# A planned attention and feed-forward kernel: the softmax of its first two tiles in two parts by heads

## Chip, cores and metric

The kernel runs on one core of a Trainium2 chip. The metric is the device time of one execution in microseconds, lower is better. All times below are microseconds unless a unit is given.

## What is computed

```python
# q, k, v: (8 batches, 8 heads, 576 tokens, 64); w_in (512, 2048), w_out (2048, 512), all float32
k_p = k.reshape(B, H, 72, 8, D).mean(axis=3)           # keys and values pooled by 8: 72 of each
v_p = v.reshape(B, H, 72, 8, D).mean(axis=3)
scores = scale * np.matmul(q, k_p.transpose(0, 1, 3, 2))
scores = scores - np.max(scores, axis=-1, keepdims=True)
attn = np.exp(scores)
attn = attn / (np.sum(attn, axis=-1, keepdims=True) + 1e-09)
attn_out = np.matmul(attn, v_p)                        # -> x: (4608 tokens, 512)
h = x @ w_in
sp = np.maximum(h, 0.0) + np.log1p(np.exp(-np.abs(h)))
out = (h * erf(sp)) @ w_out
```

## The kernel before

The 4608 tokens are nine chunks of 512. Attention goes by units of 256 tokens, two tiles of 128 each (`unit`, with `softmax_tile` for the tiles and `part` for the products with the values). Eight heads are held as four pairs (`NP` = 4), two heads of a pair in the two halves of the 128 partitions.

For a batch, `keys` loads five transfers and sums each over the 8 tokens of a pool on VectorE (L594): one of 256 KB for each of the four pairs, with that pair's first 64 pooled keys, and a last one of 128 KB with the remaining 8 pooled keys of all pairs (L605). The tile `ks` keeps them under five keys of dependence, 0 to 3 for the pairs and 4 (`NP`) for the last 8. `values` does the same for the values, on VectorE or GpSimd (L590, L592), and makes the rounded values `vb` with their remainders (L618, L622).

`softmax_tile` loads a query tile (L644, 256 KB), multiplies it with the pooled keys (`scores`, 32 small matmuls, L653) into two PSUM banks, one for each half of the heads, takes from each bank the maximum over 72 keys (L661) and subtracts it (L677) on VectorE, runs one sigmoid over all 576 columns on ScalarE (L681; with a bias of -20 it is an exponential), sums over the keys (L683), inverts (L688) and multiplies (L691, on VectorE or GpSimd). Two copies (`bb`, through L450 or L451) gather the columns left over, then the tile is transposed on TensorE (L698 for the four pairs, L699 for bb) and copied back as `et` (L708, L710) and `etb` (L715, L716). `part` multiplies them with the values (L746 with et, L752 with etb and vb), and for chunk 0 the results are split into a rounded part on ScalarE (L766) and a remainder on VectorE (L767), the tiles x.

For the feed-forward part each weight tile of 128x512 comes as 64-bit floats (L501, 512 KB), is converted by ScalarE (`cv`, L504), ScalarE or GpSimd (`low`, L508, L510) and VectorE (L512), and split into a rounded part and a remainder (`halves`, L450, L451, L462). Matmuls of weights run three products for each pair of operands (`three`, `pairs`, L819). Chunk 0 goes through w_in directly (`plain_in`): the first four weight tiles have their matmuls in two halves of 256 tokens, so that the first unit's x suffices to begin. The other chunks go through a product scheme with fewer multiplications, two chunks at a time, with sums of weights and activations that the vector engines make.

The order of all this is not that of the code. `op` notes each operation with its engine, an estimated cost, a priority (its due time) and what it reads, writes and holds; a dependence can be on a whole buffer or on one key of it. `Program.order` places the operations eight times, each time with priorities from the last placing's latest times, keeps the shortest, then moves priorities around at places that the numbers in `MOVES` draw (each is a seed of a local random shift), and emits the result. Every engine's queue, SyncE's with all transfers included, gets its order from there, and runs it in order. Where the plan leaves TensorE idle in the first 57 us, small matmuls on the constants fill in (`filler`, L1129). A changed operation, due time or list of seeds therefore changes the order in the whole kernel.

Of the kernel before, what the change touches and what calls it, by code (L numbers as in the profile page):

```python
# [402 lines left out]
def moe_attention(ctx: ExitStack, tc: tile.TileContext, cst, qa, kl, vl, wi, wo, out):  # L403
# [30 lines left out]
    def dve(n):  # L434
        return 1.15 * (n + 66) / 0.96
# [162 lines left out]
    def keys(b, base):  # L598

        ks = keys_of[b] = buf("ks", [NP, SP])  # L600
        n = P * D * POOL
        for p in range(NP):
            load_pool(kl[b, n * p:n * p + n], lambda p=p: ks.ap[:, p, :D], (ks, p),
                      base + KEYS + KEYS_R * p, "k", (D,))
        load_pool(kl[b, n * NP:], lambda: ks.ap[:, :, D:], (ks, NP), base + KEYS + KEYS_R * NP, "k", (NP, SP - D))  # L605
# [19 lines left out]
    def unit(ck, u0, tiles, parts, moment):  # L625
# [9 lines left out]
        def softmax_tile(at, r):  # L635
# [13 lines left out]
            def scores():  # L649
                for p in range(NP):  # L650
# [518 lines left out]
```

## Time and profile before

| | |
|---|---|
| time, median of 3 runs | 783.02 (782.98 to 784.59) |
| profiled execution | 783.03, its span 781.3 |
| TensorE (PE) busy | 774.1, 99% |
| VectorE (DVE) busy | 640.1, 82% |
| ScalarE (ACT) busy | 544.8, 70% |
| GpSimd (POOL) busy | 438.9, 56% |
| bytes moved by DMA | 207.66 MB, mean 266 GB/s |
| granted TensorE clock | 1.0 of full speed in all slices |

The span is the time from the first to the last instruction of the profiled execution; about 1.7 us lie around it. A busy time is the union of an engine's instructions, and for TensorE it holds the fillers as well as the work. Shares over the whole span hide that the start is another stage than the rest: up to some 26 us the first two tiles of attention and the first weights are made ready, and from there matmuls of weights follow each other. The rows further down are therefore mostly of the first 26 us.

### The profile page before, as it was taken

Reading aid. Unit: us, or ns where it says so; the run is one execution under the profiler, and the core shown is the slowest. Engines: PE = TensorE matmul, PEld = TensorE weight load, DVE = VectorE, ACT = ScalarE, POOL = GpSimd, SP = SyncE. Lnnn points to the kernel's source line nnn. Section 1 sums busy time; section 2 is a strip of 40 time slices with the busy share of each in tenths; the row PEclk is TensorE's granted clock in tenths of the full one; section 3 lists DMA queues with packets and bytes.
Section 4 is the critical chain, followed back from the end, with each engine's and each line's share of the span. In section 5 each row is a group of like instructions: output and inputs, shape, how many; then the busy total and the mean of one; then the engine's idle time right before and its main releaser. Section 6 shows DMA issues by size and latency. Waiting matters only on the chain.

```text
span 781.3 us, 15278 instructions
## 1 busy us (share of the span) xinstructions
PE 774.1 (99%) x5206; PEld 665.1 (85%) x5206; DVE 640.1 (82%) x1101; ACT 544.8 (70%) x843; POOL 438.9 (56%) x413
## 2 busy tenths in 40 slices
PE   8999999999999999999999999999999999999998
PEld 6888887888888888888888888888888888888887
DVE  6999998778888896798888898877899876667982
ACT  3999986798865752899766436879855447988730
POOL 4989892578586800476653733757916404561710
PEclk9999999999999999999999999999999999999999
DMA  9989999999999899983384889644546797447551
GB/s 332 377 279 317 347 328 359 363 346 349 353 332 385 284 374 328 386 278 135 117 320 142 258 269 361 240 162 162 190 162 197 247 296 269 137 166 264 177 188 55
DMA packets 125293, 207.66 MB, mean 266 GB/s; under 512 B 12320, under 2 KB 44448, under 8 KB 125216
## 3 DMA queue, kind: packets, MB, share of 16 engines
q1 hardware_dynamic: 125216, 206.69, 76.5%
q8 instruction: 42, 0.69, 0.4%
q14 instruction: 35, 0.29, 0.1%
HBM read 160.50 MB, written 46.14 MB: 264 GB/s over the span
## 4 chain that ended last, share of the span: by engine, by line
PE 95%; DMA 2%; ACT 1%; SPq 0%; DVE 0%; POOL 0%; issue 0%; DVEq 0%; ACTq 0%
PE o L819 43%; PE h L819 42%; PE att L746 2%; PE att L653 2%; PE att L752 2%; PE att L698 2%; DMA d<-wi 1%; DMA d<-wo 1%; DMA v<-vl 1%; PE att L1129 1%; PE att L699 1%; SPq L582 0%; POOL bb L451 0%; ACT cv L504 0%; DVE m L661 0%
## 5 line engine op out<-in xcount | busy, mean ns | idle before, releaser
L819 PE MATMUL o<-gl,w 128*128 128x512 f32 x1536 | 341.6, 381 | 0.0
L819 PEld LDWEIGHTS o<-gl,w 128*128 128x128 f32 x1536 | 287.5, 189 | 41.6 <-POOL w L462 0.4
L819 PE MATMUL h<-x,w 128*128 128x512 f32 (+1 forms) x1392 | 298.1, 373 | 0.0
L819 PEld LDWEIGHTS h<-x,w 128*128 128x128 f32 x1392 | 254.1, 189 | 34.7
L846 POOL TENSOR_TENSOR g<-d,g 128x512 f32<-128x512 f32 x73 | 93.5, 1299 | 103.5 <-ACT d L842 54.2
L450 ACT ACTIVATE gl<-g 128x512 fp32r<-128x512 f32 x183 | 108.5, 624 | 51.1 <-DVE g L989 22.1
L462 DVE TENSOR_TENSOR gl<-g,gl 128x512 fp32r<-128x512 f32 x149 | 114.9, 799 | 4.2 <-ACT gl L450 3.0
L462 POOL TENSOR_TENSOR gl<-g,gl 128x512 fp32r<-128x512 f32 x59 | 85.0, 1445 | 53.6 <-ACT gl L450 53.2
L926 DVE TENSOR_TENSOR g<-t,h 128x512 f32<-128x512 f32 x96 | 65.4, 684 | 29.1 <-PE h L819 28.5
L989 POOL TENSOR_TENSOR g<-g 128x512 f32<-128x512 f32 x37 | 65.2, 1762 | 25.3 <-ACT gl L450 11.5
L842 ACT ACTIVATE d<-d 128x1024 f32<-128x1024 f32 x72 | 73.5, 1052 | 0.5
L838 ACT ACT_TABLE_LOAD x46 | 59.0, 1283 | 17.8 <-PE h L819 13.6
L838 ACT ACTIVATE d<-g 128x512 f32<-128x512 f32 x103 | 59.1, 622 | 3.8 <-DVE g L926 3.5
L926 DVE TENSOR_TENSOR t<-t,h 128x512 f32<-128x512 f32 x57 | 39.1, 686 | 27.6 <-PE h L819 25.3
L450 ACT ACTIVATE x<-xr 128x512 fp32r<-128x512 f32 (+2 forms) x51 | 27.9, 565 | 36.9 <-DVE xr L793 33.4
L842 ACT ACT_TABLE_LOAD x41 | 52.6, 1283 | 0.7
L819 PE MATMUL h<-x,ws 128*128 128x512 f32 x192 | 43.2, 379 | 0.0
L681 ACT ACTIVATE s<-s,cst 128x576 f32<-128x576 f32 x36 | 27.5, 772 | 22.2 <-DVE s L677 22.2
L989 DVE TENSOR_TENSOR g<-g 128x512 f32<-128x512 f32 x59 | 41.7, 715 | 0.6
L819 PEld LDWEIGHTS h<-x,ws 128*128 128x128 f32 x192 | 36.3, 189 | 5.2
L462 POOL TENSOR_TENSOR x<-xr,x 128x512 fp32r<-128x512 f32 (+2 forms) x16 | 22.0, 1392 | 25.7 <-ACT x L450 25.7
L451 POOL TENSOR_SCALAR bb<-s 128x64 f32<-128x64 f32 x33 | 11.8, 365 | 42.1 <-DVE s L691 28.8
(107 smaller groups left out, 973.2 us busy)
## 6 DMA issues: line engine op xcount, KB each, us to landing
w<-ws SPq DMA_DIRECT2D x192, 256.0 KB, 4.9
w<-wo SPq DMA_DIRECT2D x128, 256.0 KB, 3.7
w<-wi SPq DMA_DIRECT2D x96, 256.0 KB, 5.3
ws<-ws SPq DMA_DIRECT2D x64, 256.0 KB, 5.0
v<-vl SPq DMA_DIRECT2D x40, 256.0 KB, 5.3
q<-qa SPq DMA_DIRECT2D x36, 256.0 KB, 5.2
out<-f SPq DMA_DIRECT2D x35, 256.0 KB, 2.6
k<-kl SPq DMA_DIRECT2D x32, 256.0 KB, 5.4
```

What stands on the lines that cost most here:

```text
L450: op("ACT", act(n), prio, lambda: nc.scalar.activation(dst(), src(), AF.Copy, scale=scale), *access, turn=turn, alt=("POOL", 0.833 * n + 1 ...
L462: both(True, dve(n), gps(n), prio + 0.1, lambda e: e.tensor_sub(lo(), src(), f32(hi())), reads + [hikey], [lokey])
L653: nc.tensor.matmul(pss[x].ap[r0:r0 + 64, SP * p:SP * p + SP], raw.ap[h:h + 64, p, r0:r0 + 64], ks.ap[h:h + 64, p], start=p == 0, stop=True ...
L681: op("ACT", act(H * SP) + 93, r + 0.8, lambda: nc.scalar.activation(s.keys[:T], s.keys[:T], AF.Sigmoid, bias=bias[0][:T], scale=1.0 / 64.0 ...
L698: nc.tensor.transpose(pa.ap[:, P * p:P * p + T], s.keys[:T, p, SP - 64:SP + 64], ident[:T, :T])
L746: nc.tensor.matmul(pd.ap[64 * y:64 * y + 64, 256 * i:256 * i + n], vs.ap[h, p], et.ap[h, p, es], start=i == 0, stop=False, skip_group_chec ...
L819: nc.tensor.matmul(o, u, v, start=first and q == 0, stop=last and q == 2, skip_group_check=True)
L838: nc.scalar.activation(y(k), hs[k][0].ap, AF.Softplus)
L842: op("ACT", act(1024), prio + 0.2, lambda k=k: nc.scalar.activation(ys[k].ap, ys[k].ap, AF.Erf), own[2 * k:2 * k + 2], own[2 * k:2 * k + 2 ...
L846: both(True, dve(512), gps(512), prio + 0.3, lambda e, k=k, h=h: e.tensor_mul(h.ap, y(k), h.ap), [own[k], h], [h])
L926: op("DVE", dve(512), prio, lambda: nc.vector.tensor_add(dst.ap, u.ap, o.ap), [u, o], [dst])
L989: both(True, dve(512), gps(512), prio, lambda e: e.tensor_sub(out.ap, u.ap, v.ap), [u, v], [out])
```

## The change

For the first unit of chunk 0 alone (tiles 0 and 1), the softmax is done in two parts of two head pairs each. The score matmuls become two operations of 16, the first of which depends on the keys 0, 1 and 4 of `ks` and the second on 2, 3 and 4; maxima and subtractions become eight passes of 144 columns in place of four of 288 (two maxima and two subtractions in each part); the sigmoid becomes two of 288 columns, and the sum over keys two. The inversion and all behind it stay whole. Banks, maxima, probabilities and sums get keys of dependence by part, so that a part's operations need not wait for the other's.

For batch 0 the due time of the last 8 keys' transfer is half a step earlier: 3.5 steps in place of 4, where the pairs have 0 to 3. And `MOVES` has a new list of seeds, longer than the old, so that the order of all engines is another one in the whole kernel.

```diff
-    43000190, 43000454, 43000917, 43001956, ...
+    41000008, 41000438, 41001345, 41006004, ...
...
-        load_pool(kl[b, n * NP:], lambda: ks.ap[:, :, D:], (ks, NP), base + KEYS + KEYS_R * NP, "k", (NP, SP - D))
+        load_pool(kl[b, n * NP:], lambda: ks.ap[:, :, D:], (ks, NP), base + KEYS + KEYS_R * (NP if b else 3.5), "k", (NP, SP - D))
...
+            split = 2 if first and u0 == 0 and not on_act else 1
+            w = NP // split
+
+            def scores(p0=0, p1=NP):
+                for p in range(p0, p1):
...
+            if split == 1:
+                op("PE", 550, r, scores, [raw, *(ks for ks, _ in rows)], pss, [s, m, z],
+                   turn="q", step=True)
+            else:
+                for p0 in range(0, NP, w):
+                    op("PE", 550 / split, r + 0.1 * p0, lambda p0=p0: scores(p0, p0 + w),
+                       [raw, *((ks, e) for ks, _ in rows for e in (*range(p0, p0 + w), NP))],
+                       [(ps, p0) for ps in pss], [s, m, z], turn="q", step=True)
+            for g, p0 in [(g, p0) for p0 in range(0, NP, w) for g in range(2)]:
+                ps, q = pss[g], r + 0.1 * p0
+                pv = lambda ps=ps, p0=p0: ps.ap[:T, SP * p0:SP * (p0 + w)].rearrange("p (h k) -> p h k", k=SP)
+                gs = slice(4 * g + p0, 4 * g + p0 + w)
+                bk, mk, sk = (ps, (m, g), (s, g)) if split == 1 else ((ps, p0), (m, (g, p0)), (s, (g, p0)))
+                op("DVE", dve(w * SP), q + 0.4, lambda pv=pv, gs=gs: nc.vector.tensor_reduce(
+                    m.ap[:T, gs], pv(), AX.X, ALU.max), [bk], [mk])
...
+                    op("DVE", dve(w * SP), q + 0.5, lambda pv=pv, gs=gs, g=g, p0=p0: nc.vector.tensor_sub(
+                        s.keys[:T, p0:p0 + w, SP * g:SP * g + SP], pv(), m.ap[:T, gs].unsqueeze(2).broadcast_to([T, w, SP])),
+                       [bk, mk], [sk])
+            if split > 1:
+                for p0 in range(0, NP, w):
+                    ps_, q = slice(p0, p0 + w), r + 0.1 * p0
+                    both_ = [(s, (g, p0)) for g in range(2)]
+                    op("ACT", act(2 * w * SP) + 93, q + 0.8, lambda ps_=ps_: nc.scalar.activation(
+                        s.keys[:T, ps_], s.keys[:T, ps_], AF.Sigmoid, bias=bias[0][:T], scale=1.0 / 64.0), both_, both_, funcs="sigmoid")
+                    op("DVE", dve(2 * w * SP + 8), q + 1.0, lambda ps_=ps_: nc.vector.tensor_reduce(
+                        z.ap[:T].rearrange("t (x p) -> t p x", x=2)[:, ps_], s.heads[:T, ps_], AX.X, ALU.add), both_, [(z, p0)])
+            elif not on_act:
```

## Rows read from the trace of the kernel before

**Rows 1.** The page, busy time, share of the span and instructions of each engine.
```profile
PE 774.1 (99%) x5206; PEld 665.1 (85%) x5206; DVE 640.1 (82%) x1101; ACT 544.8 (70%) x843; POOL 438.9 (56%) x413
```

**Rows 2.** Busy us (count) by stretch: PE, PEld, DVE, ACT, POOL; clock; DMA share; GB/s.
```profile
25.79:777.50 751.71, 750.95 (x4910) 646.35 (x4907) 619.98 (x1057) 531.23 (x814) 423.97 (x384) 1.00 0.77 264
...
8.00:17.00 9.00, 9.00 (x187) 7.73 (x186) 7.88 (x20) 3.82 (x7) 6.56 (x12) 1.00 1.03 397
17.00:26.00 9.00, 8.94 (x90) 7.34 (x89) 8.67 (x20) 8.49 (x22) 8.08 (x10) 1.00 1.04 398
```

**Rows 3.** The fillers' line: durations in ns, first and last start.
```profile
L1129 PE MATMUL att<-cst x127: 272/273/421, 2.6 to 25.2; 128*128 128x256 bf16 x127
```

**Rows 4.** Timeline of TensorE: start, length, line, tiles, count.
```profile
8.09 0.73 PE L653 MATMUL att<-ks,q 64*64 64x72 f32 x32
...
18.55 0.33 PE L699 MATMUL att<-cst,bb 128*128 128x128 f32 x1
18.72 2.02 PE L1129 MATMUL att<-cst 128*128 128x256 bf16 x17
20.67 1.09 PE L746 MATMUL att<-et,vs 64*64 64x256 f32 x16
21.70 0.73 PE L752 MATMUL att<-etb,vb 64*128 64x256 f32 x8
...
25.79 2.92 PE L819 MATMUL h<-x,w 128*128 128x256 f32 x24
```

**Rows 5.** Three of SyncE's issues, and KB and us to landing of the same three.
```profile
3.54 0.43 SPq L644 DMA_DIRECT2D q<-qa  x1
...
9.26 0.33 SPq L501 DMA_DIRECT2D d<-wi  x1
...
10.09 0.33 SPq L501 DMA_DIRECT2D d<-wi  x1
...
q<-qa SPq DMA_DIRECT2D x1, 256.0 KB, 4.2
...
d<-wi SPq DMA_DIRECT2D x1, 512.0 KB, 8.2
...
d<-wi SPq DMA_DIRECT2D x1, 512.0 KB, 8.6
```

**Rows 6.** VectorE: timeline, then groups by shape from 5 to 26 us.
```profile
6.11 1.65 DVE L594 TENSOR_REDUCE ks<-k 128x64 f32<-128x512 f32 x3 [0.73 <-DMA k<-kl]
...
11.21 0.82 DVE L661 TENSOR_REDUCE m<-att 128x4 f32<-128x288 f32 x2 [0.65 <-PE att L653]
...
13.81 0.71 DVE L683 TENSOR_REDUCE z<-s 128x8 f32<-128x584 f32 x1
...
24.70 1.09 DVE L767 TENSOR_TENSOR x<-att,x 128x256 fp32r<-128x256 f32 x3
...
L594 DVE TENSOR_REDUCE ks<-k 128x64 f32<-128x512 f32 x6 | 4.0, 681 | 0.7 <-DMA k<-kl 0.7
...
L594 DVE TENSOR_REDUCE ks<-k 128x32 f32<-128x256 f32 x1 | 0.4, 408 | 0.0
```

**Rows 7.** Timeline of ScalarE.
```profile
16.09 0.76 ACT L681 ACTIVATE s<-s,cst 128x576 f32<-128x576 f32 x1
17.51 0.66 ACT L504 ACTIVATE cv<-d 128x512 f32<-128x512 f32 x1 [0.66 <-DMA d<-wi]
18.09 0.41 ACT L450 ACTIVATE bb<-s 128x64 f32<-128x64 f32 x2
...
19.85 0.36 ACT L715 CAST etb<-att 128x256 fp32r<-128x256 f32 x1
```

**Rows 8.** Timeline of GpSimd.
```profile
14.56 2.29 POOL L691 TENSOR_TENSOR s<-s,z 128x576 f32<-128x576 f32 x2
...
18.89 0.73 POOL L622 TENSOR_TENSOR vb<-vm,vb 128x256 fp32r<-128x256 f32 x1 [0.59 <-ACT vb L450]
...
24.84 2.53 POOL L462 TENSOR_TENSOR w<-f,w 128x512 fp32r<-128x512 f32 x2
```

More of the change, by code (lines that the diff above doesn't have):

```diff
@@ L647, in softmax_tile @@
             pss = [bank("att") for _ in range(2)]
-            def scores():
-                for p in range(NP):
+            split = 2 if first and u0 == 0 and not on_act else 1
+            w = NP // split
+            def scores(p0=0, p1=NP):
+                for p in range(p0, p1):
                     for ks, r0 in rows:
@@ L654, in scores @@
                                              ks.ap[h:h + 64, p], start=p == 0, stop=True, skip_group_check=True)
-            op("PE", 550, r, scores, [raw, *(ks for ks, _ in rows)], pss, [s, m, z],
-               turn="q", step=True)
-            for g, ps in enumerate(pss):
-                pv = lambda ps=ps: ps.ap[:T, :4 * SP].rearrange("p (h k) -> p h k", k=SP)
-                gs = slice(4 * g, 4 * g + 4)
-                op("DVE", dve(4 * SP), r + 0.4, lambda pv=pv, gs=gs: nc.vector.tensor_reduce(
-                    m.ap[:T, gs], pv(), AX.X, ALU.max), [ps], [(m, g)])
+            if split == 1:
[13 more added lines that the diff above has]
+                    m.ap[:T, gs], pv(), AX.X, ALU.max), [bk], [mk])
                 if on_act:
@@ L676, in softmax_tile @@
                 else:
-                    op("DVE", dve(4 * SP), r + 0.5, lambda pv=pv, gs=gs, g=g: nc.vector.tensor_sub(
-                        s.keys[:T, :, SP * g:SP * g + SP], pv(), m.ap[:T, gs].unsqueeze(2).broadcast_to([T, NP, SP])),
-                       [ps, (m, g)], [(s, g)])
-            if not on_act:
+                    op("DVE", dve(w * SP), q + 0.5, lambda pv=pv, gs=gs, g=g, p0=p0: nc.vector.tensor_sub(
[10 more added lines that the diff above has]
+            elif not on_act:
                 op("ACT", act(H * SP) + 93, r + 0.8, lambda: nc.scalar.activation(
```

44 rows, old and new, of the table MOVES are left out of this document.

## Prediction

> **What bounds the kernel now.** The reader should look at the page's first part, then at TensorE's busy time by stretch, then at the engines' timelines ahead of the first weight matmul. The page has TensorE busy for 99% of the span [rows 1], which by itself would leave nothing to win. But 127 of its matmuls are fillers, small products on the constants that the planner puts into gaps, and they all lie before 25.5 us [rows 3]. By stretch: from 25.79 us, where the first matmul of the weights starts, to 777.5 us TensorE is busy 750.95 of 751.71 us [rows 2], and from there to the end of the span of 781.3 us lie 3.8 us for the last sums and their store. So the span is three pieces: 25.79 us of start, 751.7 us of full TensorE, 3.8 us of tail. The change removes no product of the second piece and touches nothing of the third. What it can win is in the first, and there the question is what the matmul at 25.79 us waits for.
>
> Followed back: that matmul starts as VectorE's last x remainder ends (24.70 + 1.09 = 25.79 us) [rows 4, 6]. The x tiles come from products at 20.67 and 21.70 us, which need the transposed probabilities of both tiles of the first unit; the later of the two transposes is at 18.55 us, and between it and 20.67 us stand 17 fillers [rows 4]. It was held by the small copies bb on ScalarE at 18.09 us, and those stood in the queue behind a weight conversion (cv) that sat idle 0.66 us for its transfer: issued at 9.26 us, 8.2 us to landing, so 17.4 us [rows 5, 7]. The copies' own input, tile 1's scaled probabilities, was done about a microsecond earlier: GpSimd's two multiplications run 14.56 to 16.85 us, tile 0's and then tile 1's [rows 8]. Those follow the two softmaxes, which is what the change splits.
>
> **The change, part by part.** *Tile 1, where the split alone decides.* Now its maxima start at 11.21 us and its sums end at 13.81 + 0.71 = 14.52 us [rows 6]; between lie four passes of 288 columns on VectorE, one sigmoid of 0.76 us on ScalarE [rows 7], and the sums. The trace has no pass of 144 columns. Its bounds: half of the 0.41 us that a pass of 288 takes (two maxima take 0.82 us), so 0.20 us; and that with the fixed part on top, which two sizes of one reduction give: 681 ns for 512 columns, 408 for 256, so 135 ns for none [rows 6], 0.34 us in all. I take 0.22, near the lower end, because passes back to back overlap in the trace: three key sums of 681, 681 and 408 ns are done in 1.65 us. The sigmoid's half is taken as 0.43 us (an operation of 256 columns on that engine takes 0.36 us) [rows 7] and the half sums as 0.41 (the 256-column reduction). Then: scores of the first half end 0.33 us earlier (somewhat less than half of the 0.73 us of 32 matmuls [rows 4], as the last one's way through is not halved), so VectorE starts at 10.88 and ends its four passes at 11.76; the second half's passes end at 12.64 while ScalarE does the first half; second sigmoid 12.73 to 13.16; second sums 13.25 to 13.66. Against 14.52 that is 0.85 us earlier; with 0.34 us a pass it is no gain, with 0.20 it is 1.0.
>
> *Tile 0 and the keys.* Its scores start at 8.09 us. The five key sums end at 6.11 + 1.65 = 7.76 us and the query tile lands at 3.54 + 4.2 = 7.7 us: both gate [rows 4, 5, 6]. Loading the last 8 keys ahead of the fourth pair moves 128 KB forward, and with the query tile ahead of the fourth pair too the first half need not wait for that pair's transfer and its sum (0.68 us); but the same six transfers still end at 7.7 us, and if a key transfer is the last of them its sum comes behind it, so the second half starts at about 8.6 us. By the chain above tile 0 then has its sums at 11.5 to 11.7 us. GpSimd, busy 6.56 of 9 us in this stretch with the sums of values [rows 2], could then multiply at some 13 us between two of them, or where it does so now, at 14.56; tile 1's follows 1.15 us later (2.29 for two), at 14.2 us, or at 15.7 as now. So tile 1's multiplication ends at 15.4 us at best and 16.85 at worst.
>
> *What follows.* ScalarE does tile 2's sigmoid at 16.09 to 16.85 us [rows 7]. If bb comes right behind it, it is done at 17.3 us in place of 18.5, and the transposes, their copies, the products at 20.67 and 21.70 and the x tiles move by 1.2 us to 24.6 us. The low values' other input, vb, is there at 18.89 + 0.73 = 19.62 us [rows 8], which is early enough. What is late next is the second weight: its remainder is the first of GpSimd's two from 24.84 us, done near 26.1 us [rows 8], and the second group of twelve 256-column matmuls would want it 1.3 us after 24.6, at 25.9. That takes 0.2 us. **Gain at the start: 1.0 us.**
>
> *What it adds.* Per split tile two more maxima, two more subtractions, one more sigmoid and one more sum, and two score groups of 16 matmuls for one of 32: 12 instructions on VectorE and ScalarE more for both tiles, no byte and no column more. VectorE's four extra passes and the extra sum cost between 5 x 0 and 5 x 0.135 us = 0.7 us a tile; by the prices taken above it is 0.23 (8 x 0.22 - 4 x 0.41 for the passes, 2 x 0.41 - 0.71 for the sums). They lie in the stretch from 8 to 17 us, where VectorE is busy 7.88 of 9 us, so its 1.1 us of idle time cover two tiles at 0.23 but not at 0.7 [rows 2]. Without that cover up to 0.3 us fall on what VectorE does next, tiles 2 and 3, whose products come only behind the first weight matmuls. I cost it at nothing.
>
> The nearest row gives at most 135 ns for one more instruction [rows 6]. The Trainium skill (Perfetto Trace Analysis, section Optimizing Scalar/DVE Operations) gives about 125 ns of overhead to a VectorE instruction on PSUM and 60 ns to one on SBUF, and advises grouping where the engine is saturated and breaking up where it is not but keeps others waiting. From its figures the two tiles would add, as an estimate, 2 x (4 x 0.125 + 0.06) = 1.1 us, all the idle time of that stretch, and a pass would take 0.27 us; tile 1's sums would then come 0.45 us earlier in place of 0.85, which still lets bb in behind tile 2's sigmoid, if that one is not late itself: 782.0 to 782.4 us. No operation of 144 columns in this trace decides it.
>
> *The order.* All operations of all engines are placed by the planner from the new list of seeds, so every queue (SyncE's transfers included) is in another order for the whole kernel. In the second piece only 0.76 us of idle TensorE is left to win [rows 2], so there a new order can hardly win and may lose some tenths; between a gain of 0.5 us (fewer changes between attention and weight products) and a loss of 2 us I take zero, because the present order shows how little a plan need lose.
>
> **Sum.** Profiled execution 783.03 us = span 781.3 us + 1.7 us around it; the median of the three runs, 783.02, is the same. 783.03 - 1.0 = **782.0 us**. With tile 1 at its bounds and the second weight where it is: 781.2 to 782.8.
>
> **Rivals.** *More comes.* If GpSimd multiplies tile 0 at 13 us and bb is placed ahead of tile 2's sigmoid, only vb at 19.62 us holds the second product, which is now at 21.70: 2.05 us earlier. For it: the second weight waits mostly in queues, its transfer is there at 17.4 us. Against it: from 17 to 26 us VectorE is busy 8.67 of 9 us and TensorE's start needs that work done [rows 2], so it must all be moved into the idle time before. 781.0 us, and 780.4 with a little from the order.
>
> *Nothing comes.* The weights, not x, set the start: the copies stay behind the conversion that waits for 17.4 us, or fillers stand ahead of the products as they do now, or the second remainder stays at 26.1 us and the first gap is just moved behind twelve matmuls. 783.0 us, within 0.4.
>
> *Slower.* ScalarE takes its queue in order, and the trace shows its place: at 17.51 us a conversion held the bb copies for a transfer that came later than planned [rows 7]. The next weight lands 8.6 us behind its issue at 10.09, so at 18.7 us [rows 5]. If the new order puts its conversion and its byte copy (an operation of the same 512 columns, 0.66 us as well) ahead of bb too, bb goes from 18.09 to 19.4 or 20.0 us, and the start of TensorE is lost with it: 1.3 to 1.9 us. It decides once the copies stand behind a second weight; the split then wins nothing. 784.9 us.
>
> *The change does not do what it says*, that is, the first tile's halves start together since the order puts the query tile last: then tile 0 gains nothing and tile 1 still has its 0.85 us; this lies within the forecast.
>
> **How the numbers follow.** Forecast 0.38, more 0.30, nothing 0.17, slower 0.15. 0.2% (1.57 us), about what a measurement of this kernel tells from no change, lies at 781.45 and 784.6. Faster: nearly all of "more" (0.28) and the forecast's lower edge (0.08), 0.36. Slower: most of its rival, 0.13. Within: 0.51. The range leaves out the deepest gains (0.08) and the dearest waits (0.12): 780.4 to 784.6 us.
>
> **What would show it.** Right: the first weight matmul between 24.4 and 25.2 us, tile 1's sums done before 14 us, bb ahead of the conversion that waits, fewer fillers than 127, and from there to the last matmul 751 to 752 us. More: that matmul below 24 us. Nothing: it stays near 25.8, or starts earlier while the stretch behind it grows by as much. Wrong altogether: an idle time of ScalarE or TensorE of over 1 us with a weight's transfer as its end, or a second piece above 753 us.

## The result, and the profile after

| | before | after |
|---|---|---|
| time, median | 783.81 (782.98 to 786.64, 4 runs) | 794.91 (791.94 to 799.49, 4 runs) |
| profiled execution, its span | 783.03, 781.3 | 791.94, 790.2 |
| first weight matmul | 25.79 | 26.41 |
| from there to the last matmul | 751.7 | 760.0 |

The ratio is 1.0134 [1.0109, 1.0159]: slower by some 10 us, far outside the range. The traced execution of after is its shortest: ten executions of it, six of them from a later run, have a middle of 793.0. The page of after, then its busy time from the first weight matmul to the last (columns as in [rows 2]):

```profile
PE 777.8 (98%) x5222; PEld 665.8 (84%) x5222; DVE 653.5 (83%) x1118; ACT 535.3 (68%) x854; POOL 398.5 (50%) x389
```

```profile
26.41:786.40 759.99, 755.09 (x4929) 647.35 (x4927) 632.79 (x1064) 523.98 (x828) 382.38 (x355) 1.00 0.76 261
```

TensorE is still busy 98% of the time. The 8.9 us between the two spans are: 0.6 of later start; 4.1 of idle time in the second piece (759.99 - 755.09 = 4.90, against 0.76 in [rows 2]); 1.9 of fillers there, 19 of them (4929 matmuls against 4910) where before had none [rows 3]; and 2.2 by which the same 4910 matmuls are busy longer, which the profile doesn't split. The tail is 3.8 us in both.

*Where along the span.* A table worked out from the starts in the traces: each matmul that isn't a filler counts with its length at full clock, and what a kernel has done by a time is taken from what before has done by then. So it is how many us of work TensorE lags behind before. It is good to some tenths, as small matmuls run side by side and their length is an estimate. (new_ kernels are the changed kernel with an edit, old_ kernels the kernel before; they come below.)

```
at (us)            26   45   60   80  160  200  300  770
after             0.7  0.9  1.9  3.8  7.8  8.6  9.3  9.1
old_split_keys    0.3  0.4  0.2  0.6  1.7  2.6  2.8  2.8
old_stores_late  -0.1  0.0 -0.2  2.8  7.1  7.1  7.6  7.3
new_stores_fill   0.8  0.9  2.2  3.8  6.7  6.5  7.1  6.7
new_fill_no_raw   0.4  0.9  1.7  3.8  6.0  5.8  6.7  6.0
new_six           0.8  0.9  2.4  2.6  6.5  7.6  8.2  8.0
new_fill_six      0.7  0.9  1.9  2.4  4.3  4.3  5.0  4.5
new_three_cures   0.8  1.1  1.1  2.6  4.5  4.3 10.2  9.7
```

Nearly all of the loss (8.6 of 9.1 us) lies ahead of 200 us, while weights are read, converted and stored; from there after keeps pace. A second traced execution of after (after_again) has 9.7 us at 200 and 10.2 at 770. The places can be read as TensorE's idle times (timeline: start, us, line, operation, tiles, shape, count, [idle before <- what ended it]):

```profile
44.94 1.38 PE L1155 MATMUL h<-cst 128*128 128x256 bf16 x11
...
69.01 0.72 PE L663 MATMUL att<-ks,q 64*64 64x72 f32 x30 [0.33 <-DVE g L875]
70.20 5.42 PE L845 MATMUL h<-x,w 128*128 128x512 f32 x24 [0.46 <-POOL w L457]
...
76.73 0.89 PE L845 MATMUL o<-gl,w 128*128 128x512 f32 x3 [0.56 <-DVE f L518]
78.16 0.70 PE L845 MATMUL o<-gl,w 128*128 128x512 f32 x2 [0.55 <-DVE et L736]
```

At 44.94 us stand 11 fillers, 1.13 us, in a gap that the plan has there; eight more stand at 151 us (the planner fills gaps of over 1.2 us behind its first 57 us too). The four waits that follow cost 2.7 us by the gaps between starts, and all end with a piece that VectorE or GpSimd makes: of a weight, an activation or a transposed tile.

*SyncE's queue.* What its issues waited for from 20 to 62 us in after (engine, line <- releaser: us in all, times, longest), then a part of its timeline, then before's load that answers to the one at 57.02 us:

```profile
SPq L507 <- ACT cv L510: 11.4, 6, 3.3
SPq L507 <- POOL low L516: 7.4, 4, 3.5
SPq L507 <- DVE g L875: 5.7, 2, 5.4
```

```profile
49.20 0.83 SPq L588 DMA_DIRECT2D v<-vl  x1
57.02 0.33 SPq L507 DMA_DIRECT2D d<-wi  x1
...
57.87 0.43 SPq L537 DMA_DIRECT2D wi<-w  x1
```

```profile
43.12 0.84 SPq L501 DMA_DIRECT2D d<-wi  x2
```

A weight as loaded (d) needs one of five places, which it shares with the activations' values. In after the 16th load of w_in stands at the head of the queue until 57.02 us, and the stores of converted weights (wi<-w, L537) wait behind it. Before issues the same load as the second of the two from 43.12 us, at 43.6 us (it lands at 48.4, in after at 61.1), and puts six stores between 44.95 and 49.7 us. By 60 us the DMA engines have moved 17.9 MB in after, 19.6 in before; from 60 to 115 us they are 0.95 to 0.99 busy in both, so what is late by then finds little idle time to catch up in (before, then after; columns as in [rows 2], the DMA share is the last but one):

```profile
40.00:60.00 20.00, 20.00 (x94) 17.53 (x93) 19.11 (x29) 19.77 (x25) 17.31 (x19) 1.00 0.79 268
60.00:80.00 20.00, 19.98 (x211) 16.18 (x210) 18.21 (x35) 19.26 (x25) 18.96 (x24) 1.00 0.98 331
```

```profile
40.00:60.00 20.00, 20.00 (x128) 17.12 (x127) 16.12 (x29) 19.47 (x26) 17.38 (x19) 1.00 0.65 231
60.00:80.00 20.00, 18.09 (x142) 15.04 (x141) 15.12 (x29) 17.86 (x25) 17.16 (x20) 1.00 0.97 328
```

Late stores hold places, and engines wait for them: from 60 to 200 us some 31 us in after, all such waits added up (the two largest), and 0.5 us in before (the last line):

```profile
POOL sw L562 <- DMA wf<-f: 12.3, 2, 6.2
POOL xr L819 <- DMA wo<-w: 9.6, 1, 9.6
```

```profile
ACT x L450 <- DMA wo<-w: 0.5, 1, 0.5
```

### The profile page after: what moved, and what is told of

Same layout as the page of the kernel before. It is cut to its first block, busy times and chain, and to the rows that moved or that the text cites. A ratio compares the mean times of both kernels' runs of the same rounds, so it can differ in the third digit from the quotient of the medians.

```text
span 790.2 us, 15324 instructions
## 1 busy us (share of the span) xinstructions
PE 777.8 (98%) x5222; PEld 665.8 (84%) x5222; DVE 653.5 (83%) x1118; ACT 535.3 (68%) x854; POOL 398.5 (50%) x389
## 3 DMA queue, kind: packets, MB, share of 16 engines
q1 hardware_dynamic: 125216, 206.69, 75.8%
## 4 chain that ended last, share of the span: by engine, by line
PE 80%; DMA 10%; ACT 3%; SPq 3%; POOL 2%; DVE 2%; issue 1%; DVEq 0%; ACTq 0%; POOLq 0%
PE o L845 38%; PE h L845 34%; DMA wo<-w 2%; PE att L663 2%; DMA d<-wo 2%; PE att L772 2%; PE att L724 2%; DMA v<-vl 1%; DMA wi<-w 1%; PE att L1155 1%; PE att L778 1%; DMA k<-kl 1%; DMA w<-wo 1%; SPq L537 1%; DMA sw<-wf 1%
## 5 line engine op out<-in xcount | busy, mean ns | idle before, releaser
L468 DVE TENSOR_TENSOR gl<-g,gl 128x512 fp32r<-128x512 f32 x153 | 123.8, 837 | 2.6 <-ACT gl L456 2.3
L468 POOL TENSOR_TENSOR gl<-g,gl 128x512 fp32r<-128x512 f32 x55 | 76.6, 1400 | 65.9 <-ACT gl L456 65.5
L1015 POOL TENSOR_TENSOR g<-g 128x512 f32<-128x512 f32 x44 | 62.3, 1419 | 22.3 <-DVE gl L468 13.6
L456 ACT ACTIVATE x<-xr 128x512 fp32r<-128x512 f32 (+2 forms) x58 | 30.7, 556 | 30.8 <-DVE xr L819 19.2
L1015 DVE TENSOR_TENSOR g<-g 128x512 f32<-128x512 f32 x52 | 38.7, 750 | 2.4 <-POOL g L1015 2.2
L600 DVE TENSOR_REDUCE ks<-k 128x64 f32<-128x512 f32 (+1 forms) x40 | 24.3, 625 | 13.5 <-DMA k<-kl 13.3
L468 DVE TENSOR_TENSOR x<-xr,x 128x512 fp32r<-128x512 f32 (+2 forms) x53 | 33.3, 661 | 0.7 <-ACT x L456 0.6
```

Source lines behind the costliest of these rows:

```text
L456: op("ACT", act(n), prio, lambda: nc.scalar.activation(dst(), src(), AF.Copy, scale=scale), *access, turn=turn, alt=("POOL", 0.833 * n + 1 ...
L468: both(True, dve(n), gps(n), prio + 0.1, lambda e: e.tensor_sub(lo(), src(), f32(hi())), reads + [hikey], [lokey])
L600: op("DVE", dve(8 * n), prio, lambda: nc.vector.tensor_reduce(to(), t.ap, AX.X, ALU.add), [t], [t, key], alt=("POOL", gps(4 * n) + gps(2 * ...
L1015: both(True, dve(512), gps(512), prio, lambda e: e.tensor_sub(out.ap, u.ap, v.ap), [u, v], [out])
```

## Experiments: the split or the order

**old_split_keys.** The order of before on all queues, with the split put into it. The 32 score matmuls of a tile stay one operation, so the first half doesn't start ahead of the fourth pair's keys as it may in after; what is split is VectorE's and ScalarE's part:

```diff
+            def step():                     # in place of the four maxima and subtractions
+                k = len(done); done.append(k)
+                if k == 0: maxima(0)
+                elif k == 1: less_max(0); expo(0)
+                elif k == 2: maxima(2)
+                else: less_max(2)
...
+    for e in ("SP", "DVE"):                 # last 8 keys ahead of the fourth pair
+        at = [i for i, o in enumerate(ops) if not isinstance(o, tuple) and o.eng == e][3:5]
+        ops[at[0]], ops[at[1]] = ops[at[1]], ops[at[0]]
```

> The order of the kernel before on every queue, with the softmax of the first two tiles in two parts by heads in the places of the whole one, and the transfer and the sum of the last 8 keys ahead of the fourth pair's. So the change without its new order. If the order made the loss (theory 1), this stays within 1 us of the kernel before, 782.0 to 783.5 us, with the first weight matmul at 24.8 to 25.8 us. If the split itself makes it (theory 2: more instructions on VectorE, which is busy to nine tenths in the start), it is 787 us or more.

**new_whole.** The order of after, each operation whole in the place of its second part:

```diff
-                    op("PE", 550 / split, r + 0.1 * p0, lambda p0=p0: scores(p0, p0 + w),
+                    op("PE", 550 / split, r + 0.1 * p0, lambda: second_of('q', scores),
```

> The changed kernel's order on every queue, with the softmax of the first two tiles whole again: each whole operation stands where the second of its two parts stood, and the keys are in the new order. So the new order without the split. Theory 1 (the order makes the loss): 791 to 798 us as the changed kernel. Theory 2 (the split makes it): 783 to 785 us.

**old_split_bb.** old_split_keys with tile 1's copies bb moved ahead of the conversion that waits:

```diff
+    act = [i for i, o in enumerate(ops) if not isinstance(o, tuple) and o.eng == "ACT"]
+    cv, bb = act[7], act[8:10]
+    o = ops.pop(cv)
+    ops.insert(bb[1], o)
```

> The kernel before with the split softmax in its places (as in the run on the split alone) and one more thing: tile 1's two copies bb stand ahead of the weight conversion that waits for its transfer at 17.4 us on ScalarE. The prediction's step had the first weight matmul come 1.0 us earlier then, with the second weight's remainder late next. If that holds: 24.8 to 25.2 us for that matmul, 782.5 to 784 us where the kernel before has some 784. If the fillers or the weights hold it all the same: 25.6 to 26.2 us.

| | this | before beside it | ratio |
|---|---|---|---|
| old_split_keys | 784.59 (10 runs) | 784.91 | 1.0000 [0.9985, 1.0016] |
| new_whole | 796.72 (4) | 784.91 | 1.0163 [1.0130, 1.0196] |
| old_split_bb | 783.95 (10) | 783.91 | 0.9997 [0.9983, 1.0011] |

The split costs nothing that the runs tell and brings nothing in before's order; the order makes the loss, with or without the split. (The profiled execution of old_split_keys, 2.6 us above that of before, is not its usual one: its ten runs and before's have the same middle.) Why the start gains nothing is in ScalarE's timelines, old_split_keys first, then old_split_bb, and in TensorE's of old_split_bb:

```profile
17.86 0.65 ACT L504 ACTIVATE cv<-d 128x512 f32<-128x512 f32 x1 [0.56 <-DMA d<-wi]
18.44 0.41 ACT L450 ACTIVATE bb<-s 128x64 f32<-128x64 f32 x2
```

```profile
17.33 0.42 ACT L450 ACTIVATE bb<-s 128x64 f32<-128x64 f32 x2
...
19.25 0.65 ACT L504 ACTIVATE cv<-d 128x512 f32<-128x512 f32 x1 [0.30 <-DMA d<-wi]
19.84 0.58 ACT L739 ACTIVATE et<-att 128x512 f32<-128x512 f32 x1
```

```profile
18.71 2.02 PE L1160 MATMUL att<-cst 128*128 128x256 bf16 x17
20.66 1.09 PE L777 MATMUL att<-et,vs 64*64 64x256 f32 x16
```

With bb 1.1 us earlier, the next conversion waits for its transfer and the copy et behind it ends at 20.42 us; the products start at 20.66 us (20.67 in [rows 4]), right behind 17 fillers, the first weight matmul at 25.90. So TensorE's own queue holds the start: between its first scores and its first weight matmul stand 99 of before's 127 fillers, the profile lists no wait of TensorE there, and it takes 17.70 us in before, 17.65 in old_split_keys and 17.54 in old_split_bb. These two runs show what the split costs. What it would win with fewer fillers no run here shows; with ScalarE's order of old_split_bb it would be some 0.2 us at the products (20.66 - 20.42, an estimate), as et isn't there earlier.

## Experiments: stores and bytes

**new_stores_early** moves ten stores of after (2.1 MB), which stand 9 to 22 places behind a load that waits, ahead of that load in SyncE's queue; **new_stores_fill** moves 74 of those between 45 and 145 us to places ahead of loads that wait for a buffer (both in the changed kernel, each store behind the operation that makes its data; the edit of the first):

```diff
+    for ahead, moved in ((44, (53, 54)), (46, (55, 57)), (51, (60, 62, 64, 66, 71, 73))):
+        for n in moved:
+            ops.remove(sp[n])
+            ops.insert(ops.index(sp[ahead]), sp[n])
```

> The changed kernel with nothing but ten stores of converted weights (2.1 MB, data ready since 18 to 36 us) moved forward in SyncE's queue: two ahead of the weight load at 45.5 us, two ahead of the one at 46.7, six ahead of the one at 57.0, which each stand in the queue waiting for a buffer while the DMA engines run empty. Theory 1 in its form that the DMA engines are the second bound from 60 to 300 us and that the new order lets them idle ahead of it: the idle time is used, so 2.1 MB at some 340 GB/s, up to 6 us, come back: 786 to 790 us against 792 to 799, with more bytes moved by 60 us. Theory 3 (VectorE's, ScalarE's and GpSimd's queues are late by their own order, transfers only follow): no change, 791 to 798.

> The changed kernel with 74 stores of weights (ready for 10 to 50 us) moved forward in SyncE's queue, from 45 to 145 us, each into a place where the next load stands waiting for a buffer; loads keep their order among themselves, stores too. The ten stores moved alone filled the gaps up to 60 us and left those behind. Theory 1: most of the loss comes back, 785 to 789 us, and 46 to 47 MB are moved by 140 us in place of 43.5. Theory 3: 791 us or more.

**old_more_dma** puts ten copies of 256 KB within the chip's memory into before, ahead of SyncE's 61st transfer:

```diff
+    for i in range(10):
+        o = Op("SP", 0, 0, lambda i=i: nc.sync.dma_start(hbm.tile([P, 512], F32, ...), qa[...]))
+        ops.insert(ops.index(sp[60]), o)
```

> The kernel before with ten transfers more of 256 KB each, from HBM to a spare place in HBM that nobody reads, in SyncE's queue ahead of its 61st transfer (58 us). They change no other queue. If the DMA engines have no slack behind 60 us (theory 1), the time grows by what the ten take, 4 to 7 us, to 787 to 790, as idle TensorE between 60 and 200 us. If they have slack there (theory 3), within 1 us of the kernel before.

**new_no_raw, old_no_raw, new_fill_no_raw** leave out the 20 stores of raw weights (wf<-f), in after, in before, and in new_stores_fill. The sums of weights made of them later read parts of the input in their place, so these kernels do less work and give another result:

```diff
-    ... lambda: nc.sync.dma_start(raw_hbm[0][ft], f.ap), [f], [RAW[0][ft]])
+    ... lambda: None, [f], [RAW[0][ft]])
```

> The changed kernel with its order, less work: the 20 stores of the weights' raw values (256 KB each, 5.2 MB, most of them between 47 and 175 us) are left out, and the sums of weights that are made of them later read 20 other tiles of the input in their place. Nothing else moves. Theory 1 (the stores that the new order lets pile up hold SyncE's queue and the SBUF places that the engines wait for): the waits for stores between 60 and 200 us go, 784 to 788 us. Theory 3 (the engines' own queues are late): 790 us or more.

> The same 20 stores left out of the kernel before, with the same other loads. A control: that kernel's TensorE is busy throughout behind 25.8 us, so theory 1 and theory 3 both say within 1 us of it; a gain of more than 2 us would say that the stores are a bound there too.

> The changed kernel with both cures for the stores at once: those of the first 145 us moved forward into the places where SyncE's queue waits for a buffer, and the 20 stores of raw weights (5.2 MB) left out, so that the sums of weights read input tiles in their place (this part of the computation is not what the reference does). If stores and the bytes behind them make most of the loss, what is left is the later start (0.7), the gap with 11 fillers (1.1) and about 1 us of stalls: 786 to 787. If the engines' own order makes the larger part, the two cures overlap and the time is no better than with the raw stores left out alone: 788.5 to 789.5.

**old_stores_late** is the other way round, before with 42 of its stores moved back:

```diff
+    behind = {57: (49, 50, 51), 59: (52,), 64: (58,), 68: (60,), 69: (62,), 72: (63, 65, 66, 67), ...}
+    for load, stores in behind.items():
+        for n in stores:
+            ops.remove(sp[n])
+            ops.insert(ops.index(sp[load]), sp[n])
```

> The kernel before, with only SyncE's queue changed: 42 stores of converted weights and of sums (256 KB each) that start between 45 and 157 us there are moved behind as many loads as they stand behind in the changed kernel, or as far as their readers allow; no engine's own order changes and no byte is added. If the place of the stores in SyncE's queue is a cause by itself, the kernel before gets slower by 2 to 5 us (786 to 789), with idle time of ScalarE, GpSimd or VectorE between 60 and 160 us that stores end, and TensorE behind by that much at 160 us. If the engines' own order is the cause and late stores only go along with it, it stays within 0.5 us of 783.9.

| | this | before beside it | ratio |
|---|---|---|---|
| new_stores_early | 794.35 (4 runs) | 784.91 | 1.0141 [1.0124, 1.0158] |
| old_more_dma | 789.48 (4) | 784.91 | 1.0066 [1.0051, 1.0081] |
| new_stores_fill | 791.09 (5) | 783.91 | 1.0095 [1.0064, 1.0127] |
| new_no_raw | 788.92 (6) | 783.91 | 1.0061 [1.0037, 1.0086] |
| old_no_raw | 782.14 (10) | 783.91 | 0.9984 [0.9968, 1.0001] |
| new_fill_no_raw | 789.29 (4) | 784.28 | 1.0065 [1.0050, 1.0080] |
| old_stores_late | 791.55 (4) | 784.28 | 1.0096 [1.0079, 1.0113] |

*Sufficient.* In before, moving stores back and nothing else costs 7 us (2 to 5 were expected), where the whole change costs 9 to 11, and it brings the engines' waits for stores with it. In its traced execution some 1.8 us of that are matmuls at a lower clock, by the gaps between starts: behind a wait of TensorE that ends at 150.67 us its granted clock was 0.58 from 152 to 154 us and 0.57 to 156, where it stayed at 1.00 in after. Its chain of waits (start, us, what) from 62.5 us, and what TensorE waits for:

```profile
62.58 5.12 DMA wi<-w
...
71.14 5.34 DMA wi<-w
...
77.23 1.27 POOL w L462
```

```profile
78.54 1.13 PE L819 MATMUL o<-gl,w 128*128 128x512 f32 x4 [2.84 <-POOL w L462]
```

A store that starts at 71.14 us ends at 76.48; only then has GpSimd a place for the rounded weight and its remainder, and TensorE, which wanted them at 75.7, stands still for 2.84 us. old_more_dma shows that bytes alone can do the like (5 us): a query tile lands late and holds TensorE for 3.85 us at 72.88.

*Not the whole.* Moved forward in after, the stores give back about 2 to 4 us (ten of them nothing: new_stores_early), left out they give back 4 to 6, and both together no more than the one: 789.3, where its rival theory (the engines' own order) stood at 788.5 to 789.5. new_stores_fill too came out at its rival's mark (791 or more), and new_no_raw between the two. In before leaving them out brings 1.3 us by the ratio, and its interval reaches to nothing. In new_stores_fill only 4.0 us of waits for stores are left, yet it is 3.8 us behind at 80 us, like after. So some 5 us (789.29 against 784.28) have another cause.

## Experiments: places of the loads, and the gap

In new_fill_no_raw the chain from 44 us on is one of loads: DVE g frees a place at 45.1, d<-wi lands 52.9, GpSimd's low frees it at 57.2, d<-wo lands 66.5, ScalarE's conversion follows, and TensorE waits at 75.8 us. **new_six** gives loads and activations a sixth place up to 80 us (place 7 of the others, whose three buffers go elsewhere), **new_fill_six** does it in new_stores_fill:

```diff
+            if first >= 377:
+                ok = [p for p in range(6) if ends.get(p, (0, 0))[0] < first and (p < 5 or (last < 545 and end < 84000))]
+                b.place = min(ok, key=lambda p: ends.get(p, (0, 0))[1])
...
+            if b.place == 5:
+                b.home, b.place = "u", 7
```

> The changed kernel with a sixth place for weights as loaded and for the activations' values (they share five of 4 KB a partition), from the 14th weight load on and up to about 80 us; three other buffers move to make room, no operation changes its place in a queue. If loads that wait for one of the five places are what makes TensorE stall at 68 to 78 us (2.7 us in four stalls), the 14th load is issued near 41 us in place of 45.5, the 16th and the second of w_out 2 to 4 us earlier than 57.0 and 60.5, the four stalls lose at least 1.5 us, and the stores queued behind these loads come earlier as well: 791 to 793.5. If the conversions' own place in the engines' order decides, the loads come earlier, the stalls stay and so does the time: 794 to 795.

> The same sixth place in the kernel whose stores of the first 145 us are moved forward (791.1 without the sixth place). If the loads' places are the second cause beside the stores, the stalls at 68 to 78 us shrink here too and the two cures add: 788.5 to 790. If stores in front of the loads take the time that the place gives, or the engines' own order decides, it stays within 0.7 us of 791.1.

**new_no_late_fillers** leaves out all 19 fillers behind 26 us (its edit is below), **new_three_cures** does it in new_fill_six. **new_no_gap** and **new_all_cures** take out the eight fillers at 151 us but only three of the 11 at 44.94, so they don't test what their expectations say:

```diff
+    for i in [i for i, o in enumerate(ops) if isinstance(o, tuple)][:123:-1]:
+        del ops[i]
```

> The changed kernel without the 11 fillers at 44.94 us (1.13 us from the first of them to the next weight matmul, whose operands were done at 42.4 us and whose bank was free at 44.7 us); nothing else changes. If the lag that TensorE takes up there is kept to the end, as the trace has it, the time falls by 1.0 to 1.1 us, to about 793.8. If TensorE runs ahead of the converted weights behind it anyway, it waits for them later instead and the time stays within 0.3 us of 794.9.

> The changed kernel with all three cures: stores of the first 145 us moved forward, a sixth place for weights and activations up to 80 us, no fillers behind 26 us. If the three causes are separate, the gap's 1.0 us comes off the 788.6 of the first two: 787.3 to 788.0, with some 0.7 us of later start and 2 us of small stalls left. If TensorE is held by its operands again as soon as the gap is gone, 788.3 to 789.

> The changed kernel without any of the 19 fillers behind 26 us: the 11 at 44.94 us (new_no_gap, by its edit, had left out only three of them and the eight at 151 us) and the 8 at 151.48 us. The weight matmul behind the first group then starts some 1.0 us earlier, near 45.0 us, where its bank is free. If TensorE keeps what it gains, the time falls by 1.0 to 1.5 us below the changed kernel's (its ten runs so far have a middle of 793.0): 791.5 to 792. If converted weights and stored sums are what it waits for behind that, as the stalls at 68 to 78 us suggest, the stalls grow by the same and the time stays within 0.5 us of 793.0.

> The kernel with its stores moved forward and the sixth place (788.6), without the 19 late fillers. If causes are separate: 787.0 to 787.8. If the gap is only filled by other waits: 788.2 to 789. In some executions VectorE's second multiplication near 256 us may take over 5 us behind GpSimd's row of operations, as in the profiled executions of new_whole and new_all_cures; such an execution is some 5 us longer under either theory.

The base for these is the changed kernel once more:

> The changed kernel unaltered, in more runs beside those of the other kernels: its first four runs lie between 791.9 and 799.5, so the middle of them is not known to better than some 2 us, and the gains of the cures are taken from it. By the ledger of TensorE's work (8.9 us behind in the profiled execution) 792 to 795.

| | this (lowest to highest) | before beside it | ratio |
|---|---|---|---|
| after_again | 792.9 (792.28 to 796.37, 6 runs) | 783.54 | 1.0122 [1.0099, 1.0146] |
| new_six | 791.13 (790.86 to 795.0, 5) | 783.36 | 1.0109 [1.0090, 1.0129] |
| new_fill_six | 788.58 (787.42 to 789.29, 5) | 783.36 | 1.0068 [1.0054, 1.0081] |
| new_no_gap | 793.39 (792.23 to 793.49, 4) | 784.28 | 1.0114 [1.0099, 1.0129] |
| new_no_late_fillers | 794.56 (792.78 to 796.4, 5) | 785.03 | 1.0114 [1.0088, 1.0141] |
| new_all_cures | 789.82 (787.92 to 794.94, 6) | 783.54 | 1.0087 [1.0056, 1.0119] |
| new_three_cures | 790.15 (787.0 to 793.65, 11) | 785.03 | 1.0063 [1.0041, 1.0085] |

Against the ten runs of after (middle 793.0) the sixth place gives back 1.9 us, by the ratios 1 to 2, which is near the noise: the intervals overlap. In new_stores_fill it gives 2.5 more, and no run of the one lies among those of the other. The load that stood until 57.02 us is issued at 54.78, the second of w_out at 57.19 (60.5), and TensorE's waits at 76 and 78 us are gone (new_six):

```profile
75.89 0.27 PE L725 MATMUL att<-cst,bb 128*128 128x128 f32 x1
75.92 2.91 PE L845 MATMUL o<-gl,w 128*128 128x512 f32 x11
```

The two cures add, and somewhat more: at 200 us new_fill_six is 4.3 us behind, where after is 8.6, new_stores_fill 6.5 and new_six 7.6. So neither cure does the other's work: stores late in the queue, and loads held by shared places, both cost. They aren't wholly separate, as a load that waits holds the stores behind it: in new_six the store of 57.87 us is issued at 55.63.

The gap isn't a third. Without its fillers TensorE runs through from 41.62 us, but waits later (new_three_cures, then new_fill_six):

```profile
41.62 14.19 PE L845 MATMUL h<-x,w 128*128 128x512 f32 x65
...
68.67 0.72 PE L663 MATMUL att<-ks,q 64*64 64x72 f32 x30 [0.33 <-DVE g L875]
69.86 1.32 PE L845 MATMUL h<-x,w 128*128 128x512 f32 x5 [0.46 <-DVE s L695]
```

```profile
46.09 10.61 PE L845 MATMUL h<-x,w 128*128 128x512 f32 x48
...
69.96 1.32 PE L845 MATMUL h<-x,w 128*128 128x512 f32 x5 [0.88 <-DVE s L695]
```

It starts 0.87 us earlier at 55.75 us (56.62), and by 70 us has 0.1 us left of that: the score matmuls wait for VectorE, and the weight matmuls behind them for its passes, whether TensorE comes early or late. The time tells no gain: 794.56, by its ratio 0.6 to 1.6 us below after's, in intervals that overlap; in its traced execution the clock granted to TensorE was 0.80 from 2 to 14 us, and it was late from the start.

What stays open: of the 4.3 us left in new_fill_six 0.7 are the start, 1.0 is the gap or the wait that replaces it, and 0.5 comes between 60 and 80 us. Of the 1.9 between 80 and 160 us about 1.0 is three waits of 0.31 to 0.39 us by the gaps between starts (104.77 to 123.59 us, ended by GpSimd's remainders and by converted weights), and eight fillers stand there too. That these waits come from the vector engines' own order is argued, not shown. No edit that keeps the work beats the kernel before.

## Why the prediction was wrong

1. **The order: the step that failed.** "Between a gain of 0.5 us and a loss of 2 us I take zero, because the present order shows how little a plan need lose." It cost 8.3 us in the second piece (760.0 against 751.7) in the profiled execution, and the order alone makes the loss: 1.0163 without the split (new_whole), 1.0000 for the split without the order. That 0.76 us of idle time in before [rows 2] shows what is left to win, and says nothing of how steep the loss is for another order; the bound of 2 us had no row behind it. There were rows to be had: the DMA share over the second piece, 0.77 [rows 2], is a mean over a stretch that is 0.98 to 1.03 busy from 60 to 200 us, so a transfer that comes late there has no idle time to catch up in. What the runs show in place of the zero are stores late in SyncE's queue (42 of them moved back cost 7 us in before) and loads held by the five places; with both mended about half is left (4.3 of 8.6 us at 200 us in the traces), and its cause stays open in the main. The forecast's own signs for this were "a second piece above 753 us" and an idle time of ScalarE of over 1 us ended by a weight's transfer: 1.27 us at 66.60 us.
2. **The gain at the start, 1.0 us: wrong as well.** The first weight matmul is 0.6 us later in after and 0.1 to 0.3 later with the split in before's order. The step that failed is "If bb comes right behind it", by which the products and the x tiles "move by 1.2 us". In old_split_bb it does come right behind tile 2's sigmoid, and the products stay, behind fillers. The prediction let the matmul at 25.79 us wait for the last x remainder; but TensorE's queue comes to it at that time in any case, with no idle time, behind 17 more fillers and a tile's transposes (before), and in old_split_bb it starts at 25.90 us, ahead of the end of the last remainder at 26.26 (VectorE's timeline there):

```profile
23.46 2.02 PE L1129 MATMUL att<-cst 128*128 128x256 bf16 x17
...
25.76 0.27 PE L699 MATMUL att<-cst,bb 128*128 128x128 f32 x1
```

```profile
25.18 1.08 DVE L798 TENSOR_TENSOR x<-att,x 128x256 fp32r<-128x256 f32 x3
```

   So x tiles that come earlier win nothing unless the plan has fewer fillers too. After has 124 ahead of its first weight matmul in place of 127, 100 of them behind the first scores (99 in before), and the profile lists no wait of its TensorE from 8.62 us to there. Its operations are no earlier either: GpSimd's multiplication stands at 16.04 us, behind all sums of values and vb's remainder (14.56 in [rows 8]), tile 1's bb again behind a conversion, at 18.78, and 19 fillers ahead of the products, which start at 22.23 us (20.67 in [rows 4]):

```profile
16.04 2.28 POOL L717 TENSOR_TENSOR s<-s,z 128x576 f32<-128x576 f32 x2
```

```profile
18.21 0.63 ACT L510 ACTIVATE cv<-d 128x512 f32<-128x512 f32 x1
18.78 0.41 ACT L456 ACTIVATE bb<-s 128x64 f32<-128x64 f32 x2
```

```profile
20.06 2.24 PE L1155 MATMUL att<-cst 128*128 128x256 bf16 x19
22.23 1.09 PE L772 MATMUL att<-et,vs 64*64 64x256 f32 x16
```

   "Nothing comes", at 0.17, was the right case for the split alone: it names the fillers ahead of the products and the copies behind a conversion that waits.
3. **The sizes of the split: nearly right, but tile 1 is no earlier.** VectorE's timeline in old_split_keys (two passes of 144 columns in 0.51 us, pairs 0.43 apart, so 0.215 each; forecast 0.22) and in after (half sums 0.45; forecast 0.41; half a sigmoid is 0.54, forecast 0.43):

```profile
11.56 0.52 DVE L662 TENSOR_REDUCE m<-att 128x2 f32<-128x144 f32 x2
12.00 0.51 DVE L667 TENSOR_TENSOR s<-att,m 128x144 f32<-128x144 f32 x2
```

```profile
15.25 0.45 DVE L704 TENSOR_REDUCE z<-s 128x4 f32<-128x292 f32 x1
```

   A whole pass of 288 is 0.37 from the next one's start (13.29 to 13.66 us in after), so one more pass costs 0.06 us. The Trainium skill (Perfetto Trace Analysis, section Optimizing Scalar/DVE Operations) has about 0.125 us for it on PSUM; the measurement decides. Tile 1's sums still end at 15.70 us in after (15.26 in old_split_keys), not earlier than 14.52 [rows 6]: after's order puts passes of tiles 2 and 3 between.
4. **The extra operations at nothing: right,** within 0.16% (old_split_keys).
5. **The slower rival: the right kind, the wrong queue, place and size.** It was a queue in order whose head waits, but ScalarE's at 17.5 us, for a transfer, and for 1.3 to 1.9 us. What the runs show is SyncE's queue from 45 us on, where the head waits for a place, and the stores behind it keep places that the engines want.

## What to carry to other kernels

A kernel whose bound engine is busy 99% of the time can lose much by a new order even if it has nothing to win: look at the stretch where a second resource is full too (here the DMA engines from 60 us on), list what stands at the head of its queue and what stands behind it, and take the range from that. In a queue that runs in order, put ready stores ahead of a load that waits for a buffer; a store held back holds its buffer, and the engine that fills it. An edit that changes a search's result should be tried both ways, the edit in the old order and the new order without the edit: two runs settled it here. But see first whether the old order can show a gain at all: here TensorE's fillers stood in its way.

## What the runs showed of the hardware

A multiplication of VectorE that takes 0.75 us took 5.6 us in three profiled executions (new_whole, new_all_cures, new_three_cures), while GpSimd ran one operation after the other; in before the longest is 1.83. VectorE's line by form in new_three_cures (ns: shortest, median, longest), then GpSimd, then TensorE behind it and its busy time (us), granted clock, DMA share and GB/s:

```profile
L717 DVE TENSOR_TENSOR s<-s,z x29: 743/753/5620, 84.0 to 585.6; 128x576 f32<-128x576 f32 x29
```

```profile
254.53 1.31 POOL L468 TENSOR_TENSOR ws<-sw,ws 128x512 fp32r<-128x512 f32 x1
...
259.06 1.29 POOL L468 TENSOR_TENSOR gl<-g,gl 128x512 fp32r<-128x512 f32 x1
```

```profile
261.10 0.63 PE L724 MATMUL att<-cst,s 128*128 128x128 f32 x4 [1.64 <-DVE s L717]
262.51 0.30 PE L725 MATMUL att<-cst,bb 128*128 128x128 f32 x1 [0.78 <-DVE s L695]
```

```profile
262.00:264.00 2.00, 1.06 (x5) 0.81 0.35 131
264.00:266.00 2.00, 2.00 (x7) 0.50 0.00 0
```

From 254.53 to 260.35 us six operations of GpSimd follow without a gap; VectorE's pair that starts at 255.34 ends at 261.63, behind the last of them. The Trainium skill (SBUF — State Buffer, section SBUF: two separate sides) says that the two share a pair of ports as a lock that one instruction holds to its end; here VectorE waited through several. TensorE then stood still for 2.4 us by the two notes, and its granted clock fell to 0.50, the 1.2 GHz level, and was back at 1.00 by 268 us. This execution loses some 5 us there: it is 4.3 us behind at 200 us and 10.2 at 300, new_fill_six 4.3 and 5.0. That would explain why new_three_cures lies between 787.0 and 793.65, but only one of its executions was traced; whether after's longest runs have this cause is not known.
